# Rebuilding the long-convolution half of a fused block on Trainium2: row-tiled second transform, inverse in 32x32 tiles, resident tables

## The chip, the cores and the metric

One core of one Trainium2 chip. The metric is the device time of one execution in microseconds (us). Runs of one kernel mostly agree within a few tenths of a per cent to one per cent. TensorE is the matmul engine, VectorE and ScalarE do elementwise work and move matmul results out of PSUM, the matmul's output memory (this move is called evacuation), SyncE issues most DMA transfers, and 16 DMA engines carry them.

## The reference

```python
def _A_ref(q, k, v, shift_k, ssm_k, ssm_D):        # S = 2048 tokens, D = 640 channels
    k_shift = causal 4-tap convolution of k with shift_k, per channel
    kv  = k_shift * v
    y   = irfft(rfft(kv, 2*S) * rfft(ssm_k, 2*S))[:S]     # long convolution, per channel
    return q * (y + kv * ssm_D)
def _B_ref(x, w_gate, w_up, w_down):               # 640 -> 1728 -> 640
    return (sigmoid(x @ w_gate) * (x @ w_up)) @ w_down
x  = A_q
xn = layernorm(x)
return x + _A_ref(xn, k, v, ...) + _B_ref(xn, ...)
```

Everything is bfloat16 at the borders. The output is x plus two corrections; the convolution's part is so small that the comparison with the reference does not notice wrong k, v or filter data.

## The kernel before

The 4096-point transform of each channel is split into a first transform (32 points, odd frequencies), a second one (64 points, with twiddle factors in its tables), a product of spectra, a third transform (64 points back) and an inverse stage (32 points back). Channels go through in 10 groups. Between these matmuls the kernel weaves the gate/up and down matmuls of the feed-forward half, so that TensorE always has something to do. It is written against a small static planner: each operation is recorded with an estimated duration and a priority, the planner simulates the engines and queues, and its outcome fixes the order in which each engine executes its instructions. Nothing is reordered on the chip.

```python
    def load_kv(half, pri):                       # 160-byte runs: 80 channels of one token
        for g in range(G):
            dma(... ktv(half)[r0:r0 + N1, 3:3 + N2, :] <- k3[:, :, c0:c0 + HALF])
            dma(... ktv(half)[r0 + 1:r0 + N1, 0:3, :] <- k3[0:N1 - 1, N2 - 3:N2, c0:c0 + HALF])  # halo rows
            dma(... vtv(half)[r0:r0 + N1, :, :]       <- v3[:, :, c0:c0 + HALF])
    # ... cut ...
    def rec_st2(idx, pri, dp):                    # second transform: full 128-row matmuls, 64 columns
                    for kk in range(8):
                        k = 8 * kb8 + kk
                        nc.tensor.matmul(pp[:, kk, :], lhsT=Mb[:, k, 0, :], rhs=Tv[:, :, k, im, :], start=True, stop=False)
                        nc.tensor.matmul(pp[:, kk, :], lhsT=Mb[:, k, 1 + im, :], rhs=Tv[:, :, k, 1 - im, :], start=False, stop=True)
    # ... cut ...
    def rec_st4(half, pri, dp):                   # inverse: table tiles streamed from HBM, block-diagonal
                dma(... tl[bt] <- Bdram.ap()[:, 4 * i4:4 * i4 + 4])
                            nc.tensor.matmul(py[:, i, :], lhsT=tl[bt][:, i, r, :], rhs=vview(half)[:, 4 * i4 + i, r, :], ...)
            # result goes to HBM ("yd") and is read back in token layout, in 160-byte runs
```

The table of the second transform was expanded by ScalarE into block-diagonal form, because its 128 rows hold two independent blocks of 64.

Of the kernel before, what the change touches and what calls it, by code (L numbers as in the profile page):

```python
# [18 lines left out]
S = 2048  # L19
# [6 lines left out]
G = 4  # L26
# [8 lines left out]
NSUB = HALF // (2 * JS)  # L35

# [5 lines left out]
def _dft_tables():  # L42
    k1 = np.arange(K1, dtype=np.float64)
    n1 = np.arange(N1, dtype=np.float64)
    n2 = np.arange(N2, dtype=np.float64)
    k2 = np.arange(K2, dtype=np.float64)
    odd = 2.0 * k1 + 1.0
    ang = 2.0 * np.pi * np.outer(n1, odd) / 128.0
    F = np.zeros((G, N1, K1, 2, G))
    for g in range(G):  # L50
        F[g, :, :, 0, g] = np.cos(ang)
        F[g, :, :, 1, g] = -np.sin(ang)
    F = F.reshape(P, 2 * K1 * G)
    th = 2.0 * np.pi * n2[:, None, None] * (odd[None, :, None] + 128.0 * k2[None, None, :]) / 8192.0
    M = np.zeros((2, N2, K1, 2, K2))
    M[:, :, :, 0, :] = np.cos(th)[None]
    M[:, :, :, 1, :] = np.sin(th)[None]
    M = M.reshape(P, K1, 2, K2)
    ph = 2.0 * np.pi * np.outer(k2, n2) / 64.0
    A = np.zeros((2, K2, 2, 2, N2, 2))  # L60
    for p in range(2):
        A[p, :, 0, p, :, 0] = np.cos(ph)
        A[p, :, 0, p, :, 1] = np.sin(ph)
        A[p, :, 1, p, :, 0] = -np.sin(ph)
        A[p, :, 1, p, :, 1] = np.cos(ph)
    A = A.reshape(P, 2, 2 * N2 * 2)
    t = 64.0 * n1[None, :] + n2[:, None]
    fi = 2.0 * np.pi * odd[:, None, None] * t[None, :, :] / 8192.0
    B = np.zeros((K1, G, N2, 2, G, N1))
    for g in range(G):  # L70
        B[:, g, :, 0, g, :] = np.cos(fi)
        B[:, g, :, 1, g, :] = -np.sin(fi)
    B = B.reshape(P, N2, 2, P)
    W = np.zeros((P, 4), dtype=np.float32)
    for p in range(P):
        W[p, p // N2] = 1.0
        W[p, 2 + p // N2] = -1.0
    return _f16_bits(F), _f16_bits(M), _f16_bits(A), _f16_bits(B), W


class _Op:
    __slots__ = ("eng", "dur", "fn", "alloc", "pri", "seq", "deps", "users", "nleft", "ready", "start", "end",
                 "size", "touch", "turn")


class _Plan:




    BACKLOG = 3.0
    LAT = {"PE": 0.20, "ACT": 0.22, "DVE": 0.13, "SP": 0.4}

    def __init__(self, slots, free_tags):
        self.ops = []
        self.writers = {}
        self.readers = {}
        self.slots = slots
# [6 lines left out]
    def op(self, eng, dur, fn, r=(), w=(), alloc=(), pri=0.0, size=0.0, nb=0.0):  # L105
        o = _Op()
        o.eng, o.dur, o.fn, o.pri, o.size = eng, dur, fn, pri, size
        o.alloc = list(alloc)
        o.ready = nb
        o.seq = len(self.ops)  # L110
        o.deps, o.users = set(), []
        for k in r:
            o.deps.update(self.writers.get(k, ()))
        for k in w:
            o.deps.update(self.writers.get(k, ()))
            o.deps.update(self.readers.get(k, ()))
        for k in r:
            self.readers.setdefault(k, []).append(o.seq)
        for k in w:
            self.writers.setdefault(k, []).append(o.seq)  # L120
        o.touch = set()
        for k in list(r) + list(w):
            b = k[0]
            o.touch.add(b)
        o.turn = []
        for b, tag in o.alloc:
            o.touch.add(b)
            self.managed.add(b)
            if tag not in self.free_tags:
                o.turn.append((tag, self.count.get(tag, 0)))  # L130
# [6 lines left out]
    def run(self, make):  # L137
        ops = self.ops
        for o in ops:
            o.deps.discard(o.seq)  # L140
            o.nleft = len(o.deps)
            o.end = None
            for d in o.deps:
                ops[d].users.append(o.seq)
# [4 lines left out]
        engs = ("PE", "ACT", "DVE", "SP")  # L149
        free = {e: 0.0 for e in engs}  # L150
        pool = {e: [] for e in engs}
        for o in ops:
            if o.nleft == 0:
                pool[o.eng].append(o)
# [23 lines left out]
        while len(order) < len(ops):  # L178
            pick = None
            for e in engs:  # L180
                cand = None
                for o in pool[e]:
                    t = max(o.ready, free[e])
# [10 lines left out]
                    if e == "SP":  # L194
# [3 lines left out]
                    k = (t if t > free[e] + 0.02 else free[e], o.pri, o.seq)  # L198
# [4 lines left out]
            if pick is None:  # L203
                raise RuntimeError("no operation can be placed", occupant, [(e, [(o.alloc, o.turn, o.ready) for o in pool[e]][:6]) for e in engs])
            e, o, t = pick
            pool[e].remove(o)
            o.start = t
            for g, n in o.turn:
                turns[g] = n + 1
# [3 lines left out]
            free[e] = t + o.dur  # L213
            if e == "SP":
                free[e] = t + 0.5
# [9 lines left out]
            order.append(o)  # L225
            for u in o.users:
                p = ops[u]
                p.nleft -= 1
                lat = self.LAT[e] if (p.eng != e or e == "DVE") else 0.0
                p.ready = max(p.ready, o.end + lat)  # L230
                if p.nleft == 0:
                    pool[p.eng].append(p)
        for o in order:
# [3 lines left out]
            o.fn()  # L237
# [3 lines left out]
def kernel(  # L241
# [16 lines left out]
    x2d = A_q.flatten_outer_dims()  # L258
    k2d = A_k.flatten_outer_dims()
    v2d = A_v.flatten_outer_dims()  # L260
    o2d = out.flatten_outer_dims()
    outr = o2d.rearrange("(q p) d -> p q d", p=P)
    xr = x2d.rearrange("(q p) d -> p q d", p=P)
    k3 = k2d.rearrange("(a b) d -> a b d", b=N2)
    v3 = v2d.rearrange("(a b) d -> a b d", b=N2)
# [6 lines left out]
    Fbits, Mbits, Abits, Bbits, Wmask = _dft_tables()  # L272
# [4 lines left out]
    Wdram = nc.inline_tensor(Wmask, name="masks")  # L277
# [7 lines left out]
    make_identity(nc, ident[:])  # L285
    acc = cst.tile([P, NQ, DM], BF16, name="acc")
    wd = cst.tile([P, NFC, DM], BF16, name="wd")
    Ft = cst.tile([P, 2 * K1 * G], U16, name="Ft")
    Mb = cst.tile([P, K1, 3, P], F16, name="Mb")
    Wm = cst.tile([P, 4], F32, name="Wm")  # L290
    At = cst.tile([P, 2, 256], U16, name="At")
    Fb = Ft.bitcast(F16)
    Ab = At.bitcast(F16)
    sT = cst.tile([P, 4, CG], BF16, name="sT")
    Dt = cst.tile([P, CG], BF16, name="Dt")
    hTs = [cst.tile([P, NFC, 512], BF16, name=f"hT{i}") for i in range(2)]

    yd = dr.tile([G, S, CG], BF16, name="yd")

    SLOTS = {"w": 2, "xn": 2, "xnT": 2, "sig": 2, "st": 4, "kt": 1, "vt": 1, "ht0": 1, "ht1": 1, "kvt": 2,  # L300
             "t": 3, "T": 1, "S": 1, "Z": 1, "V": 1, "yt": 2, "B": 3, "c": 3, "g": 5}
    SHAPE = {
        "w": ([P, NC, 512], BF16), "xn": ([P, DM], BF16), "xnT": ([P, NC, 512], BF16), "sig": ([P, 512], BF16),
        "st": ([P, 4, 24], F32), "kt": ([P, 5360], BF16), "vt": ([P, 5120], BF16),
        "ht0": ([P, 16, 2, N2], BF16), "ht1": ([P, 24, 2, N2], BF16), "kvt": ([P, 2, N2, JS], BF16),
        "t": ([P, N2, 2, JS], BF16), "T": ([P, 2, JS, 2 * K1 * G], BF16), "S": ([P, 2, 2, JS * K1 * G], BF16),
        "Z": ([P, 2, JS * K1 * G], BF16), "V": ([P, N2 * 2 * HALF], BF16), "yt": ([P, 8, HALF], BF16),
        "B": ([P, 4, 2, P], F16), "c": ([P, 512], F32), "g": ([P, 512], F32),
    }
    plan = _Plan(SLOTS, ("c", "g", "t"))  # L310
    tl = plan.tiles

    def make(b, tag, i):
        shape, dt = SHAPE[tag]
        if tag == "g" and b.startswith("pst"):
            shape, dt = [P, NC, P], BF16
        pool = ps if tag in ("c", "g") else wk
        return pool.tile(shape, dt, name=f"{tag}{i}", tag=f"{tag}{i}")

    def pe(dur, fn, **kw):  # L320
        plan.op("PE", dur * 1e-3, fn, **kw)

    def act(n, fn, **kw):
        plan.op("ACT", (0.833 * n + 55) * 1e-3, fn, **kw)

    def dve(n, rate, fn, **kw):
        plan.op("DVE", (1.042 * n / rate + 70) * 1e-3, fn, **kw)

    def dma(fn, kb, run, **kw):
        plan.op("SP", 0.5, fn, size=kb * 1.024 / 360.0 * (2.0 if run < 512 else 1.0), **kw)  # L330
# [4 lines left out]
    GA, GB = 25.0, 125.0  # L335
    CA, CB = 35.0, 205.0

    def gpri(p):
        if p < GA:
            return 10.0 + p  # L340
        if p < GB:
            return CA + (p - GA) / (GB - GA) * (CB - CA)
        return CB + (p - GB)

    def cpri(f):
        return CA + f * (CB - CA)

    def load_x(q0, q1, pri):
        dma(lambda: nc.sync.dma_start(acc[:, q0:q1, :], xr[:, q0:q1, :]), 160 * (q1 - q0), 1280,
            w=[("acc", q) for q in range(q0, q1)], pri=pri)  # L350

    def load_w(n, pri):
        m = n % 7
        b = f"w{n}"
        nb = pri - 12
        if m < 6:
            f0 = 256 * m
            dma(lambda: nc.sync.dma_start(tl[b][:, :, 0:256], wgr[:, :, f0:f0 + 256]), 320, 512,
                w=[(b, 0)], alloc=[(b, "w")], pri=pri, nb=nb)
            dma(lambda: nc.sync.dma_start(tl[b][:, :, 256:512], wur[:, :, f0:f0 + 256]), 320, 512,  # L360
                w=[(b, 1)], pri=pri, nb=nb)
        else:
            dma(lambda: nc.sync.dma_start(tl[b][:, :, 0:192], wgr[:, :, 1536:1728]), 240, 384,
                w=[(b, 0)], alloc=[(b, "w")], pri=pri, nb=nb)
            dma(lambda: nc.sync.dma_start(tl[b][:, :, 256:384], wur[:, :, 1536:1664]), 160, 256,
                w=[(b, 1)], pri=pri, nb=nb)
            dma(lambda: nc.sync.dma_start(tl[b][:, :, 192:256], wur[:, :, 1664:1728]), 80, 128,
                w=[(b, 0)], pri=pri, nb=nb)

    def load_small(pri):  # L370
        dma(lambda: nc.sync.dma_start(Ft[:], Fdram.ap()), 64, 512, w=[("F",)], pri=pri)
        dma(lambda: nc.sync.dma_start(At[:], Adram.ap()), 128, 1024, w=[("A",)], pri=pri)
        dma(lambda: nc.sync.dma_start(Wm[:], Wdram.ap()), 3, 24, w=[("W",)], pri=pri)
        dve(160, 4, lambda: nc.vector.memset(Dt[:], 0.0), w=[("D",)], pri=pri)
        b = "sraw"
        for g in range(G):
            def f(g=g):
# [498 lines left out]
```

## Time and profile before

312.38 us, median of 3 runs (311.58 to 313.88).

| | before |
|---|---|
| TensorE busy by the page | 282.5 us, 91% |
| TensorE streaming (count of matmuls x start-to-start spacing) | about 265 us |
| the rest of the span ("lost") | about 45 us of 310.5 |
| DMA | 42.41 MB in 136 thousand packets |

"Lost" is, in any stretch of the timeline, the length of the stretch less the number of matmuls of each shape times the spacing at which that shape streams when nothing holds it up (0.2157 us for 512 columns, 0.136 for 320, 0.109 for 256, 56 ns for 128, 29.5 ns for the 64-column second transform, 36 ns for the 80-column inverse). Unlike the busy share it isn't flattered by modelled matmul ends or by the lower clock that TensorE is granted after it has idled.

The page of the kernel before: busy time by engine, rows of 40 slices in tenths (the span is 310.5 us, so one slice is 7.8 us; slices are counted from 0; PEclk is TensorE's granted clock), DMA totals, and the chain that ended last.

```profile
PE 282.5 (91%) x2942; PEld 186.2 (60%) x2942; DVE 189.3 (61%) x416; ACT 175.6 (57%) x362; POOL 0.7 (0%) x6
...
PE   8599639999999598999989999999998999999994
...
PEclk9699787999999899999999999999999999999999
DMA  7998999821679860470098710683903789948811
...
DMA packets 136296, 42.41 MB, mean 137 GB/s; under 512 B 110344, under 2 KB 131912, under 8 KB 136264
...
PE 49%; DMA 8%; SPq 3%; DVE 2%; issue 1%; ACT 0%; ACTq 0%; DVEq 0%
```

The DMA row stays at 7 to 9 only in the first eight slices, to about 62 us; later it is uneven. The PE row has its gaps in slices 4 and 5, while DMA is full, and at slice 13.

The same kernel's waits of TensorE (what was waited for: us in total, times, longest):

```profile
PE g_420 L679 <- DMA w_379<-in_B_w_gate_dram: 4.1, 1, 4.1
PE g_1453 L679 <- DMA w_1278<-in_B_w_up_dram: 3.8, 1, 3.8
PE g_383 L679 <- DVE hT_82 L694: 3.1, 1, 3.1
```

Two weight tiles come late, each once. By stretch, 14.8 us are lost to 31 us, 12.8 from 31 to 52, 7.7 from 52 to 126, 5.4 to 275 and about 5 in the tail.

### The profile page before, as it was taken

Reading aid. Unit: us, or ns where it says so; the run is one execution under the profiler, and the core shown is the slowest. Engines: PE = TensorE matmul, PEld = TensorE weight load, DVE = VectorE, ACT = ScalarE, POOL = GpSimd, SP = SyncE. Lnnn points to the kernel's source line nnn. Section 1 sums busy time; section 2 is a strip of 40 time slices with the busy share of each in tenths; the row PEclk is TensorE's granted clock in tenths of the full one; section 3 lists DMA queues with packets and bytes.
Section 4 is the critical chain, followed back from the end, with each engine's and each line's share of the span. In section 5 each row is a group of like instructions: output and inputs, shape, how many; then the busy total and the mean of one; then the engine's idle time right before and its main releaser. Section 6 shows DMA issues by size and latency. Waiting matters only on the chain.

```text
span 310.5 us, 7159 instructions
## 1 busy us (share of the span) xinstructions
PE 282.5 (91%) x2942; PEld 186.2 (60%) x2942; DVE 189.3 (61%) x416; ACT 175.6 (57%) x362; POOL 0.7 (0%) x6
## 2 busy tenths in 40 slices
PE   8599639999999598999989999999998999999994
PEld 3354213476858275787877777867673545567772
DVE  6960877999794289988714226261669725536531
ACT  1442076898878288678644589997873533330000
POOL 0000000000000000000000000000000000000000
PEclk9699787999999899999999999999999999999999
DMA  7998999821679860470098710683903789948811
GB/s 242 199 131 119 167 348 342 125 75 25 133 92 126 141 157 0 64 128 3 2 262 234 180 23 0 150 174 81 209 7 84 176 216 243 209 95 133 283 44 42
DMA packets 136296, 42.41 MB, mean 137 GB/s; under 512 B 110344, under 2 KB 131912, under 8 KB 136264
## 3 DMA queue, kind: packets, MB, share of 16 engines
q1 hardware_dynamic: 136264, 41.96, 63.6%
q8 instruction: 23, 0.38, 0.5%
q14 instruction: 9, 0.07, 0.1%
HBM read 36.71 MB, written 5.24 MB: 135 GB/s over the span
## 4 chain that ended last, share of the span: by engine, by line
PE 49%; DMA 8%; SPq 3%; DVE 2%; issue 1%; ACT 0%; ACTq 0%; DVEq 0%
DMA yd<-yt_4158 2%; DMA yd<-yt_2439 2%; DMA B_4060<-dftB 2%; DMA yd<-yt_4062 1%; DMA B_2420<-dftB 1%; SPq L733 1%; SPq L598 1%; PE g_4627 L707 1%; PE g_4479 L707 1%; PE g_4397 L707 1%; PE g_1926 L707 1%; PE g_1805 L707 1%; PE g_4594 L707 1%; PE g_4526 L707 1%; PE g_4363 L707 1%; PE g_4435 L707 1%
## 5 line engine op out<-in xcount | busy, mean ns | idle before, releaser
L521 PEld LDWEIGHTS <-Mb 128*128 128x128 f16 x640 | 40.2, 97 | 1.7
L523 PEld LDWEIGHTS <-Mb 128*128 128x128 f16 x640 | 39.2, 97 | 1.7
L707 PEld LDWEIGHTS <-hT_81 128*128 128x128 bf16 x224 | 21.5, 98 | 7.9
L707 PEld LDWEIGHTS <-hT_82 128*128 128x128 bf16 x224 | 21.3, 98 | 7.7
L405 ACT ACTIVATE Mb<-V_366,Wm 128x1024 f16<-128x1024 f16 x8 | 9.1, 1140 | 6.0 <-DMA V_366<-dftM 6.0
L679 PEld LDWEIGHTS <-w_379 128*128 128x128 bf16 x40 | 4.5, 115 | 12.5 <-issue 4.9
L679 PEld LDWEIGHTS <-w_150 128*128 128x128 bf16 x40 | 4.2, 108 | 8.7 <-issue 5.5
L679 PEld LDWEIGHTS <-w_113 128*128 128x128 bf16 x40 | 4.3, 108 | 6.6 <-issue 2.9
L770 PE MATMUL g_88<-sig_84,ident 128*128 128x512 bf16 x18 | 6.7, 558 | 1.4 <-POOL ident masks.py:199 1.4
L679 PEld LDWEIGHTS <-w_1278 128*128 128x128 bf16 x30 | 2.8, 103 | 6.8 <-DMA w_1278<-in_B_w_up_dram 4.1
L679 PEld LDWEIGHTS <-w_427 128*128 128x128 bf16 x40 | 3.9, 98 | 4.1
L679 PEld LDWEIGHTS <-w_3832 128*128 128x128 bf16 x40 | 3.8, 98 | 4.3
L679 PEld LDWEIGHTS <-w_3547 128*128 128x128 bf16 x40 | 3.8, 98 | 3.8
L662 ACT COPY xnT_164<-g_163 128x640 bf16<-128x640 bf16 x1 | 0.7, 692 | 9.4 <-PE g_163 L659 9.4
L679 PEld LDWEIGHTS <-w_4030 128*128 128x128 bf16 x40 | 3.7, 98 | 3.8
L475 DVE TENSOR_TENSOR t_343<-kt_110,sT 128x1024 bf16<-128x1024 bf16 x1 | 0.7, 692 | 8.4 <-DMA kt_110<-in_A_k_dram 8.4
L679 PE MATMUL g_1453<-xnT_164,w_1278 128*128 128x512 bf16 x5 | 2.3, 626 | 3.8 <-DMA w_1278<-in_B_w_up_dram 3.8
L679 PEld LDWEIGHTS <-w_586 128*128 128x128 bf16 x40 | 3.8, 97 | 3.2
L408 ACT ACTIVATE Mb<-V_366,Wm 128x512 f16<-128x512 f16 x8 | 5.7, 711 | 0.0
L679 PEld LDWEIGHTS <-w_2088 128*128 128x128 bf16 x40 | 3.8, 98 | 3.0
L679 PEld LDWEIGHTS <-w_918 128*128 128x128 bf16 x40 | 3.7, 98 | 3.0
L770 PEld LDWEIGHTS <-ident 128*128 128x128 bf16 x18 | 2.3, 134 | 5.3 <-issue 3.6
(1272 smaller groups left out, 925.9 us busy)
## 6 DMA issues: line engine op xcount, KB each, us to landing
out_dram<-acc SPq DMA_DIRECT2D x8, 320.0 KB
acc<-in_A_q_dram SPq DMA_DIRECT2D x3, 640.0 KB
wd<-in_B_w_down_dram SPq DMA_DIRECT2D x3, 480.0 KB
kt_110<-in_A_k_dram SPq DMA_DIRECT2D x4, 320.0 KB
vt_157<-in_A_v_dram SPq DMA_DIRECT2D x4, 320.0 KB
kt_1224<-in_A_k_dram SPq DMA_DIRECT2D x4, 320.0 KB
vt_1233<-in_A_v_dram SPq DMA_DIRECT2D x4, 320.0 KB
vt_3062<-yd SPq DMA_DIRECT2D x16, 80.0 KB
```

The source lines that it names most:

```text
L405: act(1024 + 200, lambda ks=ks, cs=cs, m=m: nc.scalar.activation(Mb[:, ks, 0:2, cs], view()[:, ks], ACT.Copy, scale=m), r=[(b, i // 2), (" ...
L408: act(512 + 200, lambda ks=ks, cs=cs, mn=mn: nc.scalar.activation(Mb[:, ks, 2, cs], view()[:, ks, 1], ACT.Copy, scale=mn), r=[(b, i // 2), ...
L475: dve(1024, 2, lambda: nc.vector.tensor_tensor(tl[a][:], sl(ktv(half), 0), sh(3), ALU.mult), r=kr + [("s",)], w=[(a,)], alloc=[(a, "t")], ...
L521: nc.tensor.matmul(pp[:, kk, :], lhsT=Mb[:, k, 0, :], rhs=Tv[:, :, k, im, :], start=True, stop=False)
L523: nc.tensor.matmul(pp[:, kk, :], lhsT=Mb[:, k, 1 + im, :], rhs=Tv[:, :, k, 1 - im, :], start=False, stop=True)
L598: dma(lambda i4=i4, bt=bt: nc.sync.dma_start(tl[bt].bitcast(U16)[:], Bdram.ap()[:, 4 * i4:4 * i4 + 4]), 256, 2048, w=[(bt,)], alloc=[(bt, ...
L662: act(640, lambda i=i, p_=p_: nc.scalar.copy(out=tl[X][:, :, i * P:(i + 1) * P], in_=tl[p_][:]), r=[(p_,)], w=[(X,)], pri=pri + 1)
L679: nc.tensor.matmul(tl[c][:], lhsT=tl[wb][:, k, o:o + P], rhs=tl[X][:, k, :], start=(k == 0), stop=(k == NC - 1))
L707: nc.tensor.matmul(tl[pd[i]][:, 0:320], lhsT=hT[:, fc, t4 * P:(t4 + 1) * P], rhs=wd[:, fc, 320 * i:320 * i + 320], start=(fc == 0), stop=( ...
L733: dma(lambda qs=qs, g=g: nc.sync.dma_start(xv()[:, qs, g, :], xs[:, g, qs, cs]), 160, 160, w=[(xb, j) for j in range(8 * i, 8 * i + 8)], a ...
L770: nc.tensor.matmul(tl["wps"][:], lhsT=ident[:], rhs=tl["warm"][:], start=True, stop=True)
```

## The change

Its intent: spend fewer TensorE microseconds and fewer DMA packets on the convolution.

- Second transform: the two 64-row blocks become two matmuls in different row halves of the array, meant to run at the same time; no table expansion.
- Cross-half spectrum product: real and imaginary parts lie on partition halves; the adds of the product fold into the third transform's table.
- Inverse stage: 1024 matmuls on sixteen 32x32 tiles, straight into token layout; no trip through HBM. Its table, and that of the third transform, stay resident.
- Single token blocks of 512: the weights are streamed four times, not twice. Normalised x goes to HBM and is reloaded in 5120-byte runs.
- The halo rows of k (the three tokens before each stretch of 64, which the 4-tap convolution needs) come from one small matmul in place of short loads. All planner priorities were chosen anew.

```diff
 def rec_st2(...):
-                        nc.tensor.matmul(pp[:, kk, :], lhsT=Mb[:, k, 0, :], rhs=Tv[:, :, k, im, :],
-                                         start=True, stop=False)
-                        nc.tensor.matmul(pp[:, kk, :], lhsT=Mb[:, k, 1 + im, :], rhs=Tv[:, :, k, 1 - im, :],
-                                         start=False, stop=True)
+                        for r in range(2):
+                            for b in range(2):
+                                rows = slice(64 * b, 64 * b + 64)
+                                nc.tensor.matmul(tl[cs[e]][:, b, 64 * kk:64 * kk + 64],
+                                                 lhsT=Mb[rows, k, 64 - 64 * r:192 - 64 * r],
+                                                 rhs=tl[T][rows, 2 * k + r].rearrange("p x j g -> p (x j g)"),
+                                                 start=(r == 0), stop=(r == 1))
 # ... cut ...
 def rec_st4(...):
-                            nc.tensor.matmul(py[:, i, :], lhsT=tl[bt][:, i, r, :], rhs=vview(half)[:, 4 * i4 + i, r, :], ...)
+                        for g in range(G):
+                            for q in range(4):
+                                n2 = 16 * q + 4 * u + i
+                                nc.tensor.matmul(tl[cs[g // 2]][32 * q:32 * q + 32, g % 2, 80 * i:80 * i + 80],
+                                                 lhsT=Bb[32 * g:32 * g + 32, n2, r, :], rhs=tl[V][32 * g:32 * g + 32, n2, r, :],
+                                                 start=(r == 0), stop=(r == 1), tile_position=(32 * g, 32 * q))
 # ... cut ...
 def load_kv(...):
-            dma(... halo rows of k, one short load per group ...)
+        pe(mm(240), lambda: nc.tensor.matmul(tl[c][:, 0, 0:3 * HALF], lhsT=Fb[:, 256:384],
+                                             rhs=tl[kb][:, N2:N2 + 3, :].rearrange("p n d -> p (n d)"), start=True, stop=True),
+           r=[(kb, g) for g in range(G)] + [("F",)], ...)
 # ... cut ...
+    PRM = dict(GM=128.28, C0=33.7, CD=14.0, SLK=0.15, KV0=9.28, ..., X1=11.12, X2=53.06, X3=62.3, LN1=20.02, ...)
```

## The prediction

> **What bounds it now.** The page gives PE 91% busy, and that is TensorE streaming at its own pace. From the timeline's start-to-start spacings: a 512-column matmul 0.216 us, 320 columns 0.136, 256 columns 0.109, the 64-column matmuls of the second transform 29.5 ns, the 80-column ones of the inverse stage 36 ns. Times the counts of the groups view: gate/up 540 = 116.5 us, down 448 = 61, first transform 17.5, second transform 1280 = 37.8, third 17.5, inverse 256 = 9.2, transposes 4.5: about 265 us of a 310.5 us span. Stage by stage (counts per stretch times spacing) the other 45 us are: 13 before the first gate matmul at 14.05 us; 2 cold after it; 13 in 31 to 52 us, where PE waits for weight tile w_379 (4.1 and 4.6 us in the waits), queued behind k/v loads and half-throttled besides; 6.7 in 100 to 126 us (w_1278, about 4 us); 5 at the tail; 5 scattered. Long DMA pieces (yd, dftB) head the chain of waits, but PE lost only 1.8 us in 154 to 175 us, where two lie: removing them frees little.
>
> **What the change does.**
> - Second transform: still 1280 matmuls, but 64-row pairs in different row groups and PSUM banks. The Trainium skill ("TensorE: Matmul & The Clock Gate", Part 3) says different row groups run concurrently; this trace has none. Estimate: 640 x 29.5 ns = 18.9 us, plus 20 batches with a mode switch, which drains TensorE ("TensorEngine Tiling (Array Packing)", Key Properties); a 64-column matmul lasts 190 ns here, so about 0.16 us each, 3 us. 37.8 -> 22, saves 16.
> - Inverse: 256 full matmuls become 1024 on sixteen 32x32 tiles; issue-limited, I estimate 4 to 15 us, centre 7; saves 2. Third transform: 320 of 128 columns (56 ns as the transposes), 17.9, unchanged.
> - ScalarE loses the table expansion (15 us) and inverse evacuation (12). VectorE loses the final x normalise/multiply/add (23 us), gains about 18 of PSUM multiplies and adds. Evacuations become 1024 wide, on either engine: about the same 110 us in total. Neither bounds the whole, though in the convolution stage both will be some 80% busy.
> - DMA: out go 8.4 MB of table reloads and 7.9 MB in 160-byte runs (49 thousand packets); in come 9 MB of weights (single token blocks stream them four times, not twice) and 10 MB of large-run normalised x. About 46 MB, fewer packets. The 31-row halo loads of k, which slow the first k/v load (10 to 30 us), become one matmul; the convolution should start near 35 us, not 61.
>
> **On the critical path.** TensorE's streaming: 265 -> about 247 us, all critical. Lost time 45 -> about 26: start 11, early DMA hunger 6, tail 3, rest 6.
>
> **Prediction: 273 us, range 261 to 290.** Chances: faster by over 2% 0.94, within 2% 0.04, slower 0.02.
>
> **What would show it.** Second-transform pairs starting nearly together, so a 64-matmul batch lasts about 1 us, not 1.9; inverse batch of 128 under 1 us; first convolution matmul before 40 us; no gate wait over 3 us after 60 us; PE lost time under 30 us.
>
> **What would make it wrong.** Weight loads of a pair may serialise (second transform stays at 38 us: about 288); tile instructions may cost 20 ns or more each (inverse 20 us or more); two double-bank PSUM slots may make TensorE wait on evacuation; early DMA demand may still starve TensorE and drop its clock.

## The result, and the profile after

298.59 us, median of 4 runs (295.80 to 300.86; the last counts as slow and is left out of the ratio), against 312.62 for the kernel before on the same chip. The ratio is 0.9516, with a 95% interval from 0.9458 to 0.9575. A ratio is always the mean time of one kernel's fast runs over the mean of the other's fast runs of the same rounds, so it isn't quite the ratio of the medians quoted. The experiments ran on several chips, each beside the kernel before, so where two changed kernels are compared below in us, it is by the difference of their ratios, times 312.5 us; such a difference is good to about 2 to 3 us. The direction was forecast; 273 us and the range 261 to 290 were not met: the gain is 14 us (15 by the ratio), not 39.

The page of the kernel after, the same rows (span 297.8 us, one slice is 7.4 us):

```profile
PE 261.4 (88%) x3896; PEld 169.7 (57%) x3924; DVE 208.5 (70%) x383; ACT 129.2 (43%) x163; POOL 0.7 (0%) x6
...
PE   5499349989969979997699999999999999999993
...
PEclk9589859999999999999989999999999999999999
DMA  7899999889997999999332305533380004970011
...
DMA packets 100750, 46.36 MB, mean 156 GB/s; under 512 B 63912, under 2 KB 97384, under 8 KB 100712
...
PE 47%; SPq 18%; DMA 17%; DVE 14%; issue 3%; ACTq 0%; DVEq 0%
```

The DMA row now reads 8 or 9 in nearly every slice up to about 142 us, twice as long as before, and the PE row has its gaps there: slices 4 and 5, then 11, 14, 18 and 19. From slice 19 on DMA falls to about a third in the mean, and from slice 20 PE is full. The chain that ended last goes through SyncE's queue and the DMA for 35% of the span (before: 11%). The same two stretches, first in before, then in after (us busy of PE, PEld, DVE, ACT and POOL with counts, then granted clock, mean DMA share and GB/s):

```profile
0.00:44.00 44.00, 32.01 (x143) 14.35 (x143) 29.82 (x85) 14.50 (x21) 0.70 (x6) 0.88 0.96 192
44.00:142.00 98.00, 91.07 (x1065) 61.68 (x1064) 78.12 (x164) 75.87 (x153) 0.00 (x0) 0.95 0.63 121
```

```profile
0.00:44.00 44.00, 26.20 (x172) 15.94 (x175) 24.58 (x69) 13.56 (x21) 0.70 (x6) 0.78 1.03 189
44.00:142.00 98.00, 88.75 (x1177) 57.08 (x1188) 84.83 (x169) 57.23 (x69) 0.00 (x0) 0.99 1.07 234
```

Up to 44 us the change altered the traffic little: DMA was full already and stays so (192 and 189 GB/s). From 44 to 142 us it nearly doubled it (121 to 234 GB/s).

TensorE's waits in the kernel after:

```profile
PE c L460 <- DMA kt<-in_A_k_dram: 7.4, 2, 6.1
PE c L693 <- DVE xq L676: 5.8, 2, 2.9
PE c L588 <- DVE S L576: 4.7, 3, 2.6
PE g L748 <- DMA w<-in_B_w_gate_dram: 2.6, 1, 2.6
PE g L748 <- issue: 2.1, 13, 0.2
PE g L748 <- DVE hT L717: 1.6, 1, 1.6
```

And its timeline around 40 us (start, us, engine, line, what; in brackets the idle time before and what ended it). L748 is gate/up, L460 the new halo matmul, L530 the first transform, L552 the second:

```profile
29.71 2.32 PE L748 MATMUL g<-xnT,w 128*128 128x512 bf16 x10
38.14 0.36 PE L460 MATMUL c<-kt,Ft 128*128 128x240 bf16 x1 [6.11 <-DMA kt<-in_A_k_dram]
41.11 2.74 PE L748 MATMUL g<-xnT,w 128*128 128x512 bf16 x6 [2.61 <-DMA w<-in_B_w_gate_dram]
44.07 3.46 PE L748 MATMUL g<-xnT,w 128*128 128x512 bf16 x13 [0.22 <-issue]
47.37 1.04 PE L530 MATMUL c<-Ft,kvt 128*128 128x256 f16 x8
```

The small halo matmul stands in TensorE's program order and waits 6.1 us for k; then the next weight tile is late too. The Trainium skill ("TensorE: Matmul & The Clock Gate", Part 1) says that an idle window of about 3.4 us halves the clock; the trace agrees: the granted clock is 0.62 from 32 to 44 us (0.50 in each microsecond from 35 on), and the six gate matmuls from 41.11 us take 2.74 us, where the thirteen from 44.07 us take 3.46.

Later the waits name VectorE, but VectorE had been waiting itself. Its timeline in the kernel after:

```profile
78.59 1.28 DVE L654 BATCH_NORM_STATS2 st<-acc 128x6 f32<-128x320 bf16 x3 [3.40 <-DMA acc<-in_A_q_dram]
...
133.73 0.38 DVE L486 TENSOR_TENSOR ht<-ht,Dt 128x48 bf16<-128x48 bf16 x1 [4.70 <-DMA ht<-in_A_ssm_k_dram]
```

A block of x for the third normalisation and a piece of the filter for the second half come late, VectorE executes in order, so the convolution's products behind them come late (TensorE's wait for `S`, 2.6 us at 87 us), and so does a gate product at 136 us.

The stretches of the kernel after (us busy per engine with counts, then granted clock, mean DMA share, which passes 1 where packets' records overlap, and GB/s):

```profile
14.00:32.00 18.00, 16.92 (x138) 11.68 (x136) 9.13 (x21) 8.23 (x11) 0.00 (x0) 0.90 1.09 211
32.00:44.00 12.00, 3.13 (x8) 1.14 (x9) 8.63 (x23) 0.90 (x2) 0.00 (x0) 0.62 1.21 184
...
84.00:104.00 20.00, 16.79 (x239) 10.98 (x240) 19.30 (x44) 8.46 (x10) 0.00 (x0) 1.00 0.91 191
104.00:124.00 20.00, 17.98 (x236) 11.00 (x237) 18.59 (x45) 12.04 (x15) 0.00 (x0) 1.00 1.27 188
124.00:150.00 26.00, 21.05 (x264) 13.52 (x265) 20.89 (x33) 15.00 (x20) 0.00 (x0) 0.95 0.91 203
```

From these counts, streaming is about 250 us and the lost time about 48: 16.1 to 32 us, 11.7 to 64, 15.4 to 150, 5.8 to 262, 5.0 in the tail, less 6.0 for 28 gate/up matmul records missing in this trace. The weight loads of these matmuls are all recorded (520 against 492 matmuls), and set against them some 8 of the 28 are missing between 64 and 150 us (1.7 us) and 14 from there to 262 (3.0 us). So some 13.7 us are lost between 64 and 150 us; the waits named between 84 and 150 us sum to about 10. Streaming is near what was forecast (247). The lost time was to fall from 45 to 26 and did not fall at all.

Two engines are close to full in just these stretches: the DMA engines, and VectorE (19.3 of 20 us from 84 to 104). So the rivals were:

- **Theory D**: DMA time. The 16 engines are full with short packets until 142 us, and loads land late, whoever waits for them.
- **Theory V**: VectorE time. The new PSUM multiplies and wide evacuations fill it, and TensorE waits for it.
- **Theory O**: order. The planner's cost table is too cheap for what this chip shows (its plan ends at 269.9 us; a 1024-wide evacuation was planned at 0.91 us on ScalarE and took 1.01 to 1.03; a 160-byte packet at 13 ns took 21.3), so a static order that was right in the plan is wrong on the chip.

### The profile page after: what moved, and what is told of

It is laid out like the page before. It is cut to its first block, busy times and chain, and to the rows that moved or that the text cites. A ratio compares the mean times of both kernels' runs of the same rounds, so it can differ in the third digit from the quotient of the medians.

```text
span 297.8 us, 8825 instructions
## 1 busy us (share of the span) xinstructions
PE 261.4 (88%) x3896; PEld 169.7 (57%) x3924; DVE 208.5 (70%) x383; ACT 129.2 (43%) x163; POOL 0.7 (0%) x6
## 2 busy tenths in 40 slices
DMA packets 100750, 46.36 MB, mean 156 GB/s; under 512 B 63912, under 2 KB 97384, under 8 KB 100712
## 4 chain that ended last, share of the span: by engine, by line
PE 47%; SPq 18%; DMA 17%; DVE 14%; issue 3%; ACTq 0%; DVEq 0%
PE g L748 20%; PE g L762 14%; DMA acc<-in_A_q_dram 5%; SPq L480 5%; PE c L552 3%; SPq L457 3%; PE c L613 3%; DMA wd<-in_B_w_down_dram 3%; DMA w<-in_B_w_gate_dram 3%; DMA ht<-in_A_ssm_k_dram 3%; DMA kt<-in_A_k_dram 2%; SPq L398 2%; DVE P L574 2%; DVE tb L506 2%; SPq L409 2%
## 5 line engine op out<-in xcount | busy, mean ns | idle before, releaser
L748 PE MATMUL g<-xnT,w 128*128 128x512 bf16 x492 | 117.7, 383 | 8.1 <-DMA w<-in_B_w_gate_dram 2.6
L748 PEld LDWEIGHTS <-w 128*128 128x128 bf16 x520 | 49.6, 99 | 59.0 <-issue 5.7
L762 PE MATMUL g<-wd,hT 128*128 128x320 bf16 x448 | 66.1, 302 | 0.7 <-DMA wd<-in_B_w_down_dram 0.7
L715 ACT ACTIVATE sig<-g 128x512 bf16<-128x512 f32 x52 | 31.0, 599 | 62.9 <-PE g L748 59.9
L717 DVE TENSOR_TENSOR hT<-sig,g 128x512 bf16<-128x512 bf16 x52 | 35.4, 683 | 26.9 <-PE g L748 20.2
L762 PEld LDWEIGHTS <-hT 128*128 128x128 bf16 x448 | 43.2, 99 | 17.5 <-issue 0.9
L361 ACT CAST S<-c 128x1024 bf16<-128x1024 f32 x27 | 26.6, 1014 | 29.6 <-PE c L552 29.6
L574 DVE TENSOR_TENSOR P<-S 64x1024 bf16<-64x1024 bf16 x40 | 27.4, 686 | 1.4
L364 ACT ACTIVATE T<-c 128x1024 bf16<-128x1024 f32 x19 | 19.5, 1025 | 10.8 <-PE c L530 10.8
L552 PEld LDWEIGHTS <-Mt 64*128 64x128 f16 x1280 | 19.8, 95 | 7.4 <-issue 7.4
L362 DVE CAST S<-c 128x1024 bf16<-128x1024 f32 x13 | 15.9, 1220 | 10.8 <-PE c L552 10.8
L552 PE MATMUL c<-T,Mt 64*128 64x64 bf16 x1280 | 22.1, 190 | 0.0
L509 DVE TENSOR_TENSOR ta<-ta,tb 128x1024 bf16<-128x1024 bf16 x30 | 20.7, 690 | 0.7
L589 PEld LDWEIGHTS <-P 128*128 128x128 bf16 x160 | 15.9, 99 | 1.1
```

The source lines that it names most:

```text
L361: fa = lambda: nc.scalar.copy(out=out_fn(), in_=in_fn())
L364: fa = lambda: nc.scalar.activation(out_fn(), in_fn(), ACT.Copy, scale=scale)
L509: dve(1024, 2, lambda c=c: nc.vector.tensor_tensor(tl[a][:], tl[a][:], tl[c][:], ALU.add), r=[(c,)], w=[(a,)], pri=pri)
L552: nc.tensor.matmul(tl[cs[e]][:, b, 64 * kk:64 * kk + 64], lhsT=Mb[rows, k, 64 - 64 * r:192 - 64 * r], rhs=tl[T][rows, 2 * k + r].rearrange ...
L574: dve(n, 2, lambda a=a, o=o, X=X, H=H, Q=Q: nc.vector.tensor_tensor(Q()[a], X()[a], H()[o], ALU.mult), r=sr, w=[(Z, b, h)], alloc=[(Z, "P2 ...
L589: nc.tensor.matmul(o, lhsT=tl[Z][:, b, j, :], rhs=Ab[:, 1, :], start=False, stop=True)
```

## The experiments

### e1: both halves of the second transform in one row group

First, is the planned gain in the matmuls there at all?

```diff
-                                rows = slice(64 * b, 64 * b + 64)
+                                rows = slice(0, 64)
```

> The changed kernel with one line altered: both halves of every second-transform pair use rows 0 to 63 of the array, so no two can run side by side (result wrong on purpose, order of every engine unchanged). A 64-matmul batch should go from 1.04 us back to about 1.9 us, 20 batches, +17 us of TensorE streaming. Theory 'all TensorE streaming is critical' (the prediction): time rises by 15 to 18 us, to about 315. Rival 'TensorE has slack in the first 150 us, where DMA or VectorE sets the pace' (10 of the 20 batches lie there): rises by 7 to 11 us only.

Measured: 310.38 us (two of its four runs were slow ones), ratio 0.9848 [0.9769, 0.9927]. Two batches of the second transform, first in the kernel after, then in e1 (timeline of TensorE):

```profile
52.66 1.11 PE L552 MATMUL c<-T,Mt 64*128 64x64 bf16 x64
```

```profile
55.98 2.04 PE L552 MATMUL c<-T,Mt 64*128 64x64 bf16 x64
```

So row groups do run at the same time: a batch of 64 takes 1.11 us and not 2.04, and 20 batches save 18.6 us of streaming, as the skill's "TensorE: Matmul & The Clock Gate", Part 3, has it. Time grew by 10.4 us only, which is what the rival expected (7 to 11); some 8 us of the longer batches were hidden under waits. That is a first sign that TensorE does not set the pace in the first 150 us.

### e2 and e4: take work off VectorE

e2 lets only ScalarE evacuate where the planner could choose; e4 cuts 30 adds to 64 columns (wrong data on purpose).

```diff
-            fd = lambda: nc.vector.tensor_copy(out_fn(), in_fn())
+            fd = fa          # e2: the same for the scaled copy
```

```diff
-                dve(1024, 2, lambda c=c: nc.vector.tensor_tensor(tl[a][:], tl[a][:], tl[c][:], ALU.add),
+                dve(1024, 2, lambda c=c: nc.vector.tensor_tensor(tl[a][:, 0:4], tl[a][:, 0:4], tl[c][:, 0:4], ALU.add),   # e4
```

> The 16 or so PSUM evacuations that run on VectorE (1.22 us each) are issued on ScalarE instead (1.02 us), at the same places of the order; result correct. VectorE loses about 19 us of busy time, ScalarE (43% busy) gains 17. Theory V (VectorE, 90% busy from 60 to 170 us, paces the convolution and makes TensorE wait): 4 to 8 us faster. Theory D (the DMA queues, over 90% busy until 142 us, pace it): within 2 us.

> The 30 additions of the shift convolution touch 64 columns in place of 1024 (wrong result on purpose), order unchanged: VectorE loses about 17 us of its 208 us, most of it between 45 and 170 us. Theory V: 5 to 10 us faster. Theory D: under 3 us.

Measured: e2 298.23 us, ratio 0.9535 [0.9476, 0.9593]; e4 296.75 us, ratio 0.9479 [0.9432, 0.9526]. The busy line of e2:

```profile
PE 264.7 (90%) x3924; PEld 169.6 (58%) x3924; DVE 190.4 (65%) x366; ACT 143.0 (49%) x180; POOL 0.7 (0%) x6
```

VectorE lost 18 us of work in e2 (208.5 to 190.4) and 14.5 in e4, and by the ratios the time moved by +0.6 and -1.2 us, where theory V expected 4 to 10 us less. So theory V gets no support. The test is weaker than the busy line suggests: in after only 6 of the 17 evacuations, and 20 of the 30 adds, lie between 44 and 150 us, where TensorE waits. One profile each shows some 8 us lost from 84 to 150 us, 4 to 5 less than in after, whose profiled run is the slowest of its fast ones; a small part for VectorE isn't excluded. The stronger evidence against theory V is in e6 below.

### e3 and e6: the same bytes in long runs

The k and v loads read 10,240 contiguous bytes per partition in place of 64 runs of 160 (e3); e6 does so for the filter's 128-byte runs too. Bytes, DMA instructions, buffers and waits stay the same.

```diff
-            dma(... e.dma_start(tl[kb][r0:r0 + N1, 3:3 + N2, :], k3[:, :, c0:c0 + HALF]), ...
+            dma(... e.dma_start(tl[kb][r0:r0 + N1, 3:3 + N2, :].rearrange("p n d -> p (n d)"), kflat[(c0 // HALF) * N1:..., :]), ...
```

> The k and v loads bring the same bytes into the same tiles, but from 10 KB contiguous stretches in place of 160-byte runs (wrong data on purpose); order of all engines unchanged. The 32768 packets of 160 B at 21 ns, 43.7 us of all 16 queues, should fall to under 20 us. Theory D: TensorE's loss between 32 and 44 us (10 us) nearly vanishes, the waits on k at 109 us too; 12 to 18 us faster. Theory V: the early stretch gains some 5 us, the loss between 84 and 150 us stays; 4 to 7 us faster.

> As the run with k and v in long runs (288.75 us), and the filter loads too: the 20480 packets of 128 B become long runs (wrong data on purpose, engine orders unchanged). Theory D (packets on the one DMA queue decide when k, weights and filter arrive): a further 2 to 5 us, to 284 to 287, mostly before 44 us. If DMA is no longer what holds TensorE once k and v are light: within 1.5 us of 288.75.

Measured: e3 288.75 us, ratio 0.9248 [0.9192, 0.9303]; e6 285.41 us, ratio 0.9135 [0.9072, 0.9199]. By the ratios that is 8 and 12 us less than the kernel after (10 and 13 by the medians). So e3 fell short of theory D's 12 to 18 us and exceeded theory V's 4 to 7; e6's time is as theory D had it, but its further gain did not come before 44 us. The packets of k and v took 43.7 us of all 16 queues in after and 22.9 in e3, where under 20 were expected. The halo matmul starts at 33.3 us in e3 (38.1 in after), the first transform of k*v at 42.3 (47.4). From TensorE's timeline of e3:

```profile
33.29 0.26 PE L460 MATMUL c<-kt,Ft 128*128 128x240 bf16 x1 [2.06 <-issue]
```

Lost time in e6: 15.9 to 32 us, 6.8 to 64, 3.2 to 150, 2.0 to 262 and 4.6 in the tail, 32.5 in all. The stretches of e6:

```profile
32.00:44.00 12.00, 6.94 (x30) 3.36 (x31) 11.19 (x27) 1.85 (x4) 0.00 (x0) 0.72 1.07 244
...
84.00:104.00 20.00, 19.21 (x204) 11.71 (x203) 19.46 (x49) 10.92 (x13) 0.00 (x0) 1.00 0.90 215
104.00:124.00 20.00, 19.62 (x298) 11.62 (x296) 19.60 (x34) 13.20 (x16) 0.00 (x0) 1.00 0.92 251
124.00:150.00 26.00, 25.84 (x501) 18.21 (x498) 25.57 (x40) 11.99 (x16) 0.00 (x0) 1.00 0.41 115
```

With DMA about as full to 124 us, the engines move 215 to 251 GB/s where they moved 184 to 191, and reach the light-load part about 20 us sooner (120 us, not 142). VectorE is still at 19.5 of 20 us with the same work in the same order, and TensorE is nearly full all the same (3 us lost from 84 to 150 us), so a full VectorE isn't what held it. Short packets are thus shown as one cause.

Was it the DMA engines, or SyncE, which must issue all those pieces? The issue of the small resident table (64 KB, 128 pieces) tells them apart. SyncE's timeline of the kernel after, then of e3:

```profile
28.36 2.13 SPq L806 DMA_DIRECT2D At<-dftA  x1
```

```profile
23.53 0.35 SPq L806 DMA_DIRECT2D At<-dftA  x1
```

The same 128 pieces took 2.13 us to issue behind short packets and 0.35 us without. SyncE's long issues thus fit a full queue pushing back. And in e3, with no short k and v packets left, the issue of a weight tile's second half (L409) takes 0.39 us at 27.51 us and 3.38 us at 30.65. The skill's "Perfetto Trace Analysis", section What "DMA-bound" means, reads a solid issuing track as descriptor generation; here these numbers point to back-pressure.

### e12: let two weight tiles overtake on a second queue

Rival Q: the late weight tile merely stands behind k, v and x in SyncE's first-in-first-out queue.

```diff
-    load_w(2, 9.0)
+    load_w(2, 9.0, "ACT")
-                load_w(n, gt() - PRM["WL"])
+                load_w(n, gt() - PRM["WL"], "ACT" if n == 3 else "SP")
```

> After, with weight tiles 2 and 3 issued from the ScalarE queue in place of the SyncE queue; same bytes, same packets, right result. Rival Q (the weight tile comes late at 41.1 us because it stands behind k, v and x loads in one first-in-first-out queue): the 2.6 us wait of the gate matmul for it goes, and the time falls 3 to 6 us, to 292 to 296. Theory D (the 16 DMA engines themselves are full, so whoever is served first makes another late): the gate wait may go, but the k load lands later by as much, and the time stays within 2 us of 298.4.

Measured: 304.76 us, ratio 0.9767 [0.9699, 0.9834]: 6 us slower than after by the medians, 8 by the ratios. TensorE's waits in e12:

```profile
PE c L460 <- DMA kt<-in_A_k_dram: 8.0, 2, 4.8
...
PE g L748 <- DMA w<-in_B_w_gate_dram: 4.9, 1, 4.9
```

The halo matmul slid to 42.1 us, and the late weight tile is now the next one, issued by SyncE at 41.03 us. Both expectations were missed. The run isn't a clean test of rival Q: the planner laid the whole order anew around the two tiles (1606 of TensorE's 3924 weight loads stand elsewhere; the first k load is issued at 21.16 us, not at 16.70, and the fourth weight tile, the late one of after, at 13.81, not at 35.16). What it shows is that moving these loads ahead, with the order that follows, cost more than it gained. The skill ("DMA: Bandwidth & Descriptors", Issuing engines are not separate DMA queues) says that all issuers end on the same 16 engines; this run fits that (k came 4 us later), but with the order changed it doesn't show it.

### e10: weights first, filter later

In the start, x's later rows, the filter and the first weights compete. e10 puts the first filter load behind the first weights.

```diff
-    load_h(0, 0, -2.3)
+    load_h(0, 0, 3.5)
```

> The first filter load (8 transfers, 4096 packets of 128 B) is issued after the first two weight tiles and not before; correct result. If those packets delay x and the first weights: first gate matmul at 11 to 12 us in place of 14.06, total 1 to 3 us faster. If the start is set by the normalisation chain and its activation-table load: no change at 14 us.

Measured: 300.61 us, ratio 0.962 [0.9573, 0.9668], no gain (3 us slower by the ratios; 1 to 3 us less were expected). The first gate matmul started at 8.28 us in e10, not at 14.06, so those packets did delay it. But VectorE's timeline in e10 shows what paid for it:

```profile
10.85 1.28 DVE L654 BATCH_NORM_STATS2 st<-acc 128x6 f32<-128x320 bf16 x3 [3.86 <-DMA acc<-in_A_q_dram]
```

x's next rows came at 10.85 us (8.4 in after), lost time to 32 us was 16.4 (16.1 in after), and the halo matmul waited until 40.0. So in the start, too, one load's gain was another's delay.

### e7 and e11: the planner's costs and its order

e7 gives the planner costs nearer to the measured ones and keeps all priorities; a 160-byte packet stands at 18.5 ns (the trace has 21.3), the filter's 128-byte packets stay at 11.8 (15.0). e11 has the same costs as e7, and 23 priorities searched anew in the planner (on its simulation only; the work, bytes and packets are those of after, and the result is right).

```diff
-        plan.op({"ACT": ((0.833 * n + 55) * 1e-3, fa), "DVE": ((1.042 * n + 75) * 1e-3, fd)}, **kw)
+        plan.op({"ACT": ((0.833 * n + 175) * 1e-3, fa), "DVE": ((1.042 * n + 170) * 1e-3, fd)}, **kw)      # e7, e11
-                size=nd * (7.0 + run / 26.6) / 16e3 + 0.02, **kw)
+                size=nd * (18.5 if run == 160 else 7.0 + run / 26.6) / 16e3 + 0.02, **kw)                  # e7, e11
-    PRM.update(_Plan.PRM)
+    PRM.update(GM=262.74, C0=36.6, KV0=12.04, H1=36.29, WD=45.7, X1=-2.65, X2=91.4, X3=136.05, ...)       # e11
```

> Same work, correct result: only the cost table by which the kernel lays out its order is set to the durations of the changed kernel's trace (VectorE and ScalarE instructions about 0.1 us dearer, a 160-byte packet 18.5 ns and not 13). Theory O (the stalls come from an order laid for cheaper loads and instructions: the in-order engines meet waits that a truer order would have filled): 4 to 10 us faster, 289 to 295. Theory D (the load volume itself binds, whatever the order): within 3 us of 298.6.

> As e7_plan_all_costs, and the order's priorities (when each load and stage may go) chosen anew for those costs; correct result, same instructions. Theory O: 282 to 290 us, with TensorE's loss between 32 and 44 us and 84 to 150 us cut to half or less. Theory D: not below 293.

Measured: e7 298.21 us, ratio 0.957 [0.9509, 0.9631], nothing gained; e11 290.31 us, ratio 0.9313 [0.9278, 0.9349], 6 us less than after by the ratios (8 by the medians) with the same work. Dearer costs alone didn't mend the order; another order did. Building the kernels again shows where the planner's own plans end: 269.9 us for after, 285.5 with e7's costs, 275.8 for e11, while the traces span 297.8, 297.2 and 289.7. The new costs bring the plan nearer to the chip, still 12 to 14 us short of it. Whether the search needed them isn't shown: no run searched anew on the old costs. TensorE's stretches in e11:

```profile
84.00:104.00 20.00, 19.12 (x235) 11.29 (x234) 14.10 (x43) 10.01 (x13) 0.00 (x0) 1.00 0.50 115
104.00:124.00 20.00, 19.70 (x241) 11.71 (x242) 16.98 (x28) 12.26 (x16) 0.00 (x0) 1.00 1.23 211
124.00:150.00 26.00, 25.07 (x322) 17.90 (x320) 22.66 (x41) 12.68 (x16) 0.00 (x0) 1.00 1.14 216
```

It spreads the loads (DMA share 0.50 from 84 to 104 us) and TensorE is nearly full from 64 on: 4.5 us lost between 64 and 150, where after lost some 13.7. Its start is a little worse (17.9 to 32 us). Theory O, which expected 282 to 290 us, holds for a part.

### e15: one load's priority moved by hand

In after, 640 KB of x for the second block are issued from 17.5 to 23.4 us, in the middle of the k loads. e15 puts them and their normalisation 26 us later.

```diff
-               WDS=1.98, X1=11.12, X2=53.06, X3=62.3, LN1=20.02, ...
+               WDS=1.98, X1=38.0, X2=53.06, X3=62.3, LN1=46.0, ...
```

> After, with the loads of the second row block of x (640 KB, issued from 17.5 to 23.4 us between the first and the second k load) and its normalisation put about 26 us later; nothing else is changed by hand, right result. Theory O (the order of the loads in the hungry stretch is at fault): the halo matmul comes 2 to 4 us earlier than 38.1 us, and the time falls 2 to 5 us, to 293 to 296. If displaced work only starves another load later: within 2 us of 298.4, with a new wait between 50 and 100 us.

Measured: 318.83 us, ratio 1.0211 [1.0152, 1.027], 20 us slower than after (22 by the ratios). The halo matmul did come earlier, at 34.3 us, as theory O had it; the time is a miss for both expectations. Stretches of e15:

```profile
64.00:84.00 20.00, 12.21 (x275) 9.44 (x274) 18.11 (x47) 12.48 (x13) 0.00 (x0) 0.74 1.09 280
84.00:104.00 20.00, 13.18 (x133) 10.24 (x133) 14.12 (x39) 7.96 (x10) 0.00 (x0) 0.74 0.53 120
```

22 us are lost between 64 and 104 us, with not one gate/up matmul from 64 to 84: the second token block was not ready, so TensorE had no filler between the convolution's stages (its longest wait in this run, 4.5 us, is for the reloaded normalised x), and its clock fell to 0.74. That load in the middle of the hungry stretch was there for a reason. Nor was it the only thing that moved: the planner laid the order anew around it (2001 of 3924 weight loads stand elsewhere), and its plan for e15 ends at 282.0 us, 12 later than after's, so most of the loss was in the plan. Shifting a single load by hand did not mend this order.

### e13: new order and long runs together

The edits of e11 and e6 in one kernel, wrong data on purpose.

```diff
-    PRM.update(_Plan.PRM)
+    PRM.update(GM=262.74, C0=36.6, KV0=12.04, ...)                              # and the costs of e11
-            dma(... e.dma_start(tl[kb][r0:r0 + N1, 3:3 + N2, :], k3[:, :, c0:c0 + HALF]), ...
+            dma(... e.dma_start(tl[kb][...].rearrange("p n d -> p (n d)"), kflat[...]), ...   # v and filter likewise
```

> The searched order of e11 with the k, v and filter loads of e6 in long runs (wrong data on purpose, same bytes and same order of instructions as e11). If the searched order and the shorter DMA time mend the same loss (late loads from 32 to 150 us), the two don't add: 282 to 287, about e6's 285.4. If they mend different losses, they add: 290.3 less some 10 to 13, so 276 to 281.

Measured: 282.26 us, ratio 0.9029 [0.8963, 0.9095]. The sum of both would have been 277 by the medians and 279 by the ratios. The time is at the border of the two expectations: 15 us less than after, where long runs alone gave 12 and the order alone 6, so an overlap of 3 us that isn't clear of the noise. The stretches say more: between 64 and 150 us each edit alone leaves only 3 to 4.5 us lost, so there both mend the same loss. Its chain that ended last, and its stretches:

```profile
PE 90%; DMA 4%; DVE 1%; issue 1%; SPq 1%; DVEq 0%; ACTq 0%
```

```profile
64.00:84.00 20.00, 20.00 (x293) 15.83 (x291) 17.37 (x31) 10.62 (x12) 0.00 (x0) 1.00 0.80 212
84.00:104.00 20.00, 20.00 (x179) 11.45 (x178) 17.09 (x45) 11.26 (x15) 0.00 (x0) 1.00 0.48 131
104.00:124.00 20.00, 20.00 (x265) 12.14 (x265) 17.77 (x31) 12.27 (x16) 0.00 (x0) 1.00 0.95 236
124.00:150.00 26.00, 26.00 (x450) 19.71 (x443) 22.65 (x41) 10.30 (x12) 0.00 (x0) 1.00 0.51 125
```

The chain is TensorE for 90% (47% in after), and no time is lost from 64 to 150 us. What remains lost is 33 us: 17.8 to 32 us, 6.1 to 64, 3.5 to 262, 5.9 in the tail. In time, though with wrong data, this is near the kernel that the prediction described, with a longer start.

### e14: long runs in the kernel before

```diff
-            dma(... nc.sync.dma_start(ktv(half)[r0:r0 + N1, 3:3 + N2, :], k3[:, :, c0:c0 + HALF]), ...
+            dma(... nc.sync.dma_start(ktv(half)[r0:r0 + N1, 3:3 + N2, :].rearrange("p n d -> p (n d)"), kflat[...]), ...   # v likewise
```

> The kernel before, with its k and v loads in 10 KB runs as in e3 (wrong data on purpose; its small halo loads stay as they are). If hunger for short packets is the same loss in both kernels, which the change left standing, before falls by about what after fell, 8 to 12 us, to 301 to 304. If before hides these loads better, it falls by under 4 us, to 308 to 312, and the hunger is something that the change brought.

Measured: 307.14 us, ratio 0.9849 [0.9776, 0.9921], about 5 us less than before: between the two expectations, nearer to the second. Lost from 31 to 52 us fell from 12.8 to 8.3, and from 100 to 126 from 6.7 to 4.0. Before had the hunger of the early stretch already; after gains 8 us from the same edit (10 by the medians), nearly twice as much.

### All runs

| kernel | us, median | ratio to before | what it says |
|---|---|---|---|
| after | 298.59 | 0.9516 | |
| e1 one row group | 310.38 | 0.9848 | row groups run at the same time |
| e2 evacuation on ScalarE | 298.23 | 0.9535 | no sign that VectorE sets the pace |
| e4 short adds | 296.75 | 0.9479 | the same |
| e3 k, v in long runs | 288.75 | 0.9248 | DMA packets do |
| e6 k, v, filter in long runs | 285.41 | 0.9135 | more so |
| e7 measured plan costs | 298.21 | 0.957 | dearer plan costs alone: nothing |
| e10 filter later | 300.61 | 0.962 | the start is a queue, too |
| e11 new order | 290.31 | 0.9313 | order is worth 6 to 8 us; correct, best of the correct ones |
| e12 two weights on another queue | 304.76 | 0.9767 | overtaking, in a new order, costs more than it gains |
| e13 e11 + long runs | 282.26 | 0.9029 | 15 us together, 12 and 6 apart |
| e14 before, long runs | 307.14 | 0.9849 | in before the same edit is worth about half as much |
| e15 x block later | 318.83 | 1.0211 | one priority by hand: 20 us lost |

Not tried: to stream the weights twice and not four times within this kernel, as the kernel before does. By the author's account the version that was built for it read stale weights. So how much of the hunger is due to the 9 MB of extra weights stays open.

## Why the prediction was right or wrong

**TensorE's streaming, 265 to 247 us: right.** Measured about 250. The second transform saved what was forecast (batch 1.04 to 1.11 us; e1). The third transform stayed the same. The inverse was forecast at 7 us (9.2 less the 2 saved) and took 9.3 to 9.8 (batches of 128 in 1.16 us and more, where the prediction wanted under 1): 2.5 us off.

**DMA of 46 MB in fewer packets: right in amount** (46.36 MB, 100,750 packets), and wrong in what followed from it. The prediction counted bytes and packets over the whole execution. What counts is when: nearly all of the 160-byte packets that the change took away lay after 126 us, where before lost only about 5 us up to 275; the traffic to 44 us, where DMA was full, stayed as it was (192 and 189 GB/s); and from 44 to 142 us the added loads filled the DMA engines (share 0.63 to 1.07).

**The step that failed: "Lost time 45 -> about 26: start 11, early DMA hunger 6, tail 3, rest 6."** It was about 48. Term by term:

| term | forecast | after | e13 (new order, long runs) |
|---|---|---|---|
| start, to 32 us | 11 | 16.1 | 17.8 |
| early hunger, 32 to 64 us | 6 | 11.7 | 6.1 |
| rest, 64 to 262 us | 6 | 21.2, less missing records: about 16.5 | 3.5 |
| tail | 3 | 5.0 | 5.9 |
| sum (after: less all missing records) | 26 | 48 | 33 |

- *Early hunger.* The prediction named the cause in before as loads of k and v, and laid their slowness on the halo rows: "one matmul" was to bring the convolution to 35 us. The first k*v transform started at 47.4 us. Before lost 12.8 us from 31 to 52 us, and the change left about that loss standing. The halo's packets were the small part: 32768 packets of 160 bytes stayed, and turning them into long runs brought 8 us in all (e3), with the loss from 32 to 64 us down from 11.7 to about 6.5. The halo matmul even added a place in TensorE's order that waits for k.
- *Rest.* The prediction thought of the convolution stage as "some 80% busy" engines and no wait. Instead late loads stopped VectorE, and VectorE in its order stopped TensorE. e6 shows that cheaper packets take most of this loss away, e11 that another order does; with less work for VectorE (e2 and e4) the time stayed within 2 us.
- *Start.* The prediction assumed an earlier start without a mechanism. The first gate matmul was at 14.05 us in before and 14.06 in after, and e10 shows that moving it to 8.28 us gained nothing.

**The risk was named, and not priced.** The last sentence of "what would make the prediction wrong" has it: early DMA demand may still starve TensorE and drop its clock. The clock was 0.62 from 32 to 44 us. "First convolution matmul before 40 us" held by the halo matmul (38.1 us), with the first transform of k*v at 47.4. "No gate wait over 3 us after 60 us" held, but TensorE's waits had moved to other instructions, so these tests passed while their purpose failed.

**What is shown and what is not.** Shown: TensorE gained what it should; a full VectorE isn't what held TensorE (e6); short packets are a cause (8 to 12 us of the missing 26); another order is worth 6 to 8 us with the same work. With both mended, 9 us of the forecast are still missing (282 against 273), in e13's profile (282.9) almost 10: the start is about 7 of them, the tail 3, and streaming 3, set against 2.6 better than forecast in the rest. Not shown: how much comes from streaming the weights four times, how far the packets' gain and the order's overlap in time, whether the search needed the new costs, and whether any order of loads can shorten the start.

## What to carry to other kernels

Count a DMA change by stretch and not by total: a transfer removed where the engines had room bought little here, and one added where they were full was paid for by the instruction that stood next in an in-order queue. Where TensorE waits for VectorE, look at what VectorE waited for before blaming its load. And a static order is part of the kernel: set the plan's end against the chip's (269.9 and 297.8 us here), and search the whole order again where they differ, because one priority changed by hand can lose more (20 us) than the rebuild gained.

## What the Trainium skill lacked or had wrong

- "DMA: Bandwidth & Descriptors" has no time for a short packet in a full queue. In the trace of after a 160-byte packet took 21.3 ns in the mean and a 512-byte one 32 ns; in before, with other traffic around it, the 160-byte packet took 16.8 ns.
- "Perfetto Trace Analysis", What "DMA-bound" means: an issuing track full of long DMA slices is given as a limit of its own. Here the issue of the same 128 pieces took 2.13 us or 0.35 us, with short packets before them or without: the track can, it seems, also be solid from back-pressure.
- "TensorE: Matmul & The Clock Gate", Part 3: no figure for two 64-row groups with few columns. Measured: 64 matmuls of 64 columns in 1.04 to 1.11 us against 1.97 to 2.04 in one row group. For 32x32 tiles of 80 columns it took 9 to 10 ns per matmul (128 in 1.16 to 1.23 us, in five of after's eight batches), where the page has about 4 ns of issue per tile.
- "TensorEngine Tiling (Array Packing)", Key Properties, says that a change of tiling mode drains TensorE, without a time. In after 0.16 us of idle "issue" stands before most gate matmuls that follow a tiled batch (12 of the 13 places of the "issue" line in after's waits above); that this is the drain isn't shown.
